# Moving the conditional expert tiles to the middle of the loop, splitting all operands of the dense layer ahead of it, and swapping its two passes

## The chip, the cores and the metric

The kernel runs on one core of a Trainium2 chip. TensorE (PE) multiplies and transposes, VectorE (DVE), ScalarE (ACT) and GpSimd (POOL) work on tiles in SBUF and PSUM, and SyncE (SP) issues nearly all DMA. Each engine works through its own instructions in order; semaphores order the engines among each other. The metric is the time of one execution on the device in microseconds (us). TensorE's clock has two levels here, 1.2 and 2.4 GHz; the profile gives the granted clock as a share of the upper one.

## The reference

1792 tokens (4 sequences of 448) of width 768 pass through three parts in float32:

```
scores = q @ k^T / 8 - log(448);  attn = sigmoid(scores);  x = attn @ v    # 12 heads of 64
e = argmax(x @ w_gate);  g = softmax(x @ w_gate)[e]                        # 8 experts
y = g * (relu(x @ w1[e]) @ w2[e])                                          # 768 -> 1024 -> 768
h = y @ w_in;  out = (h * sigmoid(h)) @ w_out                              # 768 -> 2048 -> 768
```

Which expert a token takes depends on the inputs, so the number of tokens of each expert is known only while the kernel runs. w_in and w_out are float64 (read as pairs of 32-bit words) and are turned into float32 on the chip, called decoding here: a `Square` on ScalarE and four operations on VectorE for each piece of 128 x 768.

## The kernel before, in words

Matrices that want float32 accuracy are split in two parts, high and low (names ending in `h` and `l`), and each product is three matmuls. A split is a cast on ScalarE and a subtraction on VectorE (a few on GpSimd).

**Experts.** Tokens are sorted by expert and padded to tiles of 128. The loop has 21 positions (`TMAX`); 14 are needed whatever the inputs (`TMIN`), the rest stand under a branch. With these inputs 19 tiles are live; tiles 0 to 13 are unconditional, 14 to 18 ran under branches, and the branch of position 19 left the loop. In one position TensorE runs 36 matmuls of the first layer (`l1`) in two halves, transposes, and 48 of the second (`l2`). After the first half and 9 more matmuls of the other one it needs ScalarE's `relu` (`hs`), later `hl` from VectorE. When the next tile has another expert, its weights are split: w1 (`split1`) at the end of the position, w2 (`split2`, five pieces and then three) early in the next, and SP starts the loads of the expert after that into `stage1` (3 MB) and `stage2`. The experts change ahead of tiles 4, 5, 6, 10, 11, 13 and 16. `EARLY` says behind which tiles pieces of w_out are decoded (`early`); results go to `Wo` in HBM through two slabs of `sqp`, in turn. `yout` scales the tile's result (`ys`) and stores it to `Yd`.

**The dense layer.** It runs in two passes over tokens, before 768 tokens in pass 0 (two columns of blocks, 384 each) and 1024 in pass 1 (512 each; a pass of W tokens here means blocks W wide), each of eight blocks j over the inner width of 2048. A block has seven products (`prod`, 9 matmuls each) by a scheme that needs seven block products for a 2 x 2 block matrix, then the output half (`ystep`). The seven operands `x` are sums and differences of token rows, transposed. They are made in chunks of 128 columns by `xprep` (gather the rows from `Yd`, transpose, add, split, `put` to `T0` or `T1` in HBM) and loaded from there. For pass 0 three chunks ran behind tiles 11, 12 and 13, with 9 puts each: two of the seven operands were split there, and the other five put whole and split at the head of the dense layer (`xsplit`, `xa`). `xprep1` made pass 1's chunks during pass 0, and `wdecode` the four pieces of w_out left by `EARLY`. `wiload` and `woload` load a block's weights (`wf`, `wof`), `wisplit` and `wosplit` split them.

All of it is recorded in the order in which the code is written (`manual_schedule`), so each engine's queue is the order of the calls; SP's queue holds loads and stores in the same way, and a store that waits for its data holds up the loads written behind it.

Of the kernel before, what the change touches and what calls it, by code (L numbers as in the profile page):

```python
# [2 lines left out]

# [41 lines left out]
WS = 384, 512  # L45
MB = 0, 6
# [13 lines left out]
def attn_moe_ffn(ctx: ExitStack, tc, qT, kT, v, wg, w1, w2, w_in, w_out, out):  # L60
# [21 lines left out]
    T0 = dp.tile([9, 128, KH, WS[0]], F32, name="T0")  # L82
# [8 lines left out]
    pg_t = cp.tile([128, TMAX], F32, name="pg_t")  # L91
    tbl = cp.tile([128, 3, TMAX], I32, name="tbl")
# [61 lines left out]
    gp = M1.pool("m_g", 2)  # L154
    gs4 = M1.pool("m_s", 4)
# [224 lines left out]
    def choose():  # L380
# [17 lines left out]
        nc.vector.tensor_scalar(out=pg_t[:, 0:1], in0=es, scalar1=float(PG), scalar2=None, op0=ALU.mult)  # L398
# [38 lines left out]
    def tables(pn):  # L437
        t3 = lambda n, w=TMAX: c2.tile([128, w, E], F32, name=n)
        t2 = lambda n, w=TMAX: c2.tile([128, w], F32, name=n)
        b3 = lambda t, w=TMAX: t.unsqueeze(1).to_broadcast([128, w, E])  # L440
        b2 = lambda t, w=TMAX: t.unsqueeze(2).to_broadcast([128, w, E])
# [43 lines left out]
        ge, oh = t3("ge"), t3("oht")  # L485
        vec.tensor_scalar(out=tcap, in0=iota_t, scalar1=tot[:, 0:1], scalar2=None, op0=ALU.min)
# [4 lines left out]
        vec.tensor_tensor(out=oh, in0=b2(tcap), in1=b3(sa), op=ALU.is_ge)  # L491
        yield 1
        vec.tensor_tensor(out=ge, in0=b2(tcap), in1=b3(se[:, 0]), op=ALU.is_ge)
        yield 1
        vec.tensor_sub(out=oh, in0=oh, in1=ge)
        yield 1
        vec.tensor_tensor(out=ge, in0=oh, in1=b3(wv), op=ALU.mult)
        yield 1
        st = t2("stt")
        vec.tensor_reduce(out=st, in_=ge, axis=AX.X, op=ALU.add)  # L500
        yield 1
        vec.tensor_add(out=pg_t, in0=st, in1=tcap)
# [49 lines left out]
    def prep(t, nt=N):  # L552
        tk = keep(gs4, [128, 1], F32, "tk", t % 4)
        jk = keep(gs4, [128, NPG], F32, "jk", t % 4)
        nc.vector.scalar_tensor_tensor(out=jk, in0=iota_pg, scalar=pg_t[:, t:t + 1], in1=tt_all,
# [4 lines left out]
        gx = keep(gp, [128, DM], F32, "gx", t % 2)  # L560
        nc.gpsimd.indirect_dma_start(out=gx, out_offset=None, in_=Xd[0:nt], in_offset=off,
# [45 lines left out]
    def rload(f):  # L607
        rawload(rawm[f % 2], w_out[:, f], nc.sync)
# [37 lines left out]
    for k in range(0, G + LAG, 2):  # L646
# [25 lines left out]
        for j in (k, k + 1):  # L672
# [93 lines left out]
    def yout(t, py, gg, tk):  # L766
# [37 lines left out]
    ne = ne1 = reg(tbl[0:1, 2, 0:1], (SP,), E - 1)  # L804
# [9 lines left out]
    def gather(m, xt):  # L814
        nr = min(m + E, TMAX) * 128
        g = nc.gpsimd.indirect_dma_start(out=xt, out_offset=None, in_=Yd[0:nr],
                                         in_offset=bass.IndirectOffsetOnAxis(ap=cidx[:, m:m + 1], axis=0),
                                         bounds_check=nr - 1, oob_is_err=False)
        for t in range(nr // 128, len(ydma)):
            tc.declare_no_dep(g.ins, ydma[t].ins, reason="the rows gathered here end before tile t's")  # L820

    def xprep(p, c, ra, rb, tmp, slab, px):
# [15 lines left out]
        def split(i, a):  # L838
            h, l = slab(), slab()
# [214 lines left out]
    def xprep1():  # L1054
# [259 lines left out]
```

## Time and profile before

| | us |
|---|---|
| median of 3 runs | 1077.64 (1077.37 to 1083.63) |
| profiled execution | 1074.67, span 1072.7 |
| PE busy | 1003.3 (94%) |
| DVE busy | 711.3 (66%) |
| ACT busy | 504.4 (47%) |
| POOL busy | 105.6 (10%) |

Attention and routing fill the first 214 us, expert tiles 1 to 18 the time to 571.7, the dense layer the rest. A busy share of 94% for PE counts a matmul at the lower clock as busy for its longer time, so the clock rows have to be read beside it. DMA moved 206 GB/s in the mean; in the expert part and at the change of pass it moved up to twice that.

### The profile page before, as it was taken

The numbers are of one execution on the slowest core, as the hardware profiler recorded it, in microseconds if no ns is written. First come the engines' busy times: TensorE is split into PE (matmuls) and PEld (weight loads), VectorE is DVE, ScalarE is ACT, GpSimd is POOL, SyncE is SP. The second block draws the span as 40 slices with busy tenths as digits, with TensorE's granted clock in tenths as the row PEclk, the third lists the DMA queues.
The fourth block names the chain that finished last, engine by engine and source line by source line (L and its number), as shares of the span: only waits on it lengthen the run. The fifth ranks groups of instructions, "written<-read, shape, count | busy, mean of one in ns | idle before, by whom it ended". The sixth has DMA issues, their size and how long they took to land. (4 is left out here: it accounts for less than half of the span.)

```text
span 1072.7 us, 15464 instructions
## 1 busy us (share of the span) xinstructions
PE 1003.3 (94%) x5410; PEld 846.8 (79%) x5410; DVE 711.3 (66%) x1388; ACT 504.4 (47%) x836; POOL 105.6 (10%) x97
## 2 busy tenths in 40 slices
PE   7999999799999999989996799989897999999996
PEld 4555555689888888878885799979895999988996
DVE  5899985945986496441612578878873366766664
ACT  6677666334873285522622554445442533344231
POOL 1000000411222023120201000100010000000002
PEclk9999999999999999989997799999999999999998
DMA  8989998367996579884816355546489221022202
GB/s 287 317 307 296 362 283 252 105 232 269 348 371 249 180 257 348 268 271 145 280 45 231 123 196 196 179 160 204 143 308 403 82 82 45 37 81 81 82 1 118
DMA packets 87673, 220.59 MB, mean 206 GB/s; under 512 B 9952, under 2 KB 51808, under 8 KB 81696
## 3 DMA queue, kind: packets, MB, share of 16 engines
q1 hardware_dynamic: 81200, 200.21, 53.4%
q0 software_dynamic: 4528, 19.29, 5.3%
q8 instruction: 44, 0.72, 0.3%
q14 instruction: 45, 0.37, 0.1%
q10 hardware_dynamic: 1856, 0.01, 0.1%
HBM read 164.60 MB, written 54.87 MB: 205 GB/s over the span
## 5 line engine op out<-in xcount | busy, mean ns | idle before, releaser
L1204 PE MATMUL y<-wo,gh 128*128 128x384 f32 x448 | 153.3, 342 | 3.0 <-ACT wo L1011 2.9
L1206 PE MATMUL y<-wo,gl 128*128 128x384 f32 x448 | 151.2, 338 | 0.0
L1205 PE MATMUL y<-wo,gh 128*128 128x384 f32 x448 | 150.9, 337 | 0.3 <-DVE wo L1012 0.3
L1215 DVE TENSOR_TENSOR acc<-acc,y 128x384 f32<-128x384 f32 x196 | 102.0, 551 | 23.3 <-PE y L1206 21.9
L758 PE MATMUL y<-w2h,hl 128*128 128x384 f32 x304 | 103.9, 342 | 10.9 <-DVE hl L747 8.8
L756 PE MATMUL y<-w2h,hh 128*128 128x384 f32 x304 | 106.1, 349 | 0.7 <-ACT hh L746 0.7
L757 PE MATMUL y<-w2l,hh 128*128 128x384 f32 x304 | 103.1, 339 | 3.7 <-POOL w2l L726 2.1
L236 ACT ACTIVATE a<-s,bias 128x896 f32<-128x896 f32 x96 | 82.8, 913 | 46.3 <-PE s L233 43.7
L731 PE MATMUL h<-w1h,xh 128*128 128x512 f32 x228 | 92.7, 407 | 0.6 <-issue 0.3
L733 PE MATMUL h<-w1h,xl 128*128 128x512 f32 x228 | 90.8, 398 | 0.4 <-DVE xl L714 0.4
L732 PE MATMUL h<-w1l,xh 128*128 128x512 f32 x228 | 90.6, 397 | 0.0
L1204 PEld LDWEIGHTS y<-wo,gh 128*128 128x128 f32 x448 | 84.8, 189 | 6.0 <-ACT wo L1011 3.4
L1004 DVE TENSOR_TENSOR wl<-wf,wh 128x384 fp32r<-128x384 f32 x110 | 60.7, 553 | 37.8 <-ACT wh L1003 37.8
L1206 PEld LDWEIGHTS y<-wo,gl 128*128 128x128 f32 x448 | 84.7, 189 | 1.2 <-DVE gl L1117 1.2
L1205 PEld LDWEIGHTS y<-wo,gh 128*128 128x128 f32 x448 | 84.8, 189 | 1.0 <-DVE wo L1012 0.7
L249 PE MATMUL o<-a,vf 128*64 128x448 f32 x384 | 83.0, 554 | 0.0
L747 DVE TENSOR_TENSOR hl<-x,hh 128x512 fp32r<-128x512 f32 x38 | 26.2, 689 | 84.2 <-ACT hh L746 76.1
L758 PEld LDWEIGHTS y<-w2h,hl 128*128 128x128 f32 x304 | 57.7, 190 | 13.7 <-DVE hl L747 10.9
L757 PEld LDWEIGHTS y<-w2l,hh 128*128 128x128 f32 x304 | 57.8, 190 | 5.3 <-POOL w2l L726 2.7
L1117 DVE TENSOR_TENSOR gl<-sg,gh 128x384 fp32r<-128x384 f32 (+1 forms) x64 | 40.0, 626 | 31.9 <-ACT gh L1115 30.4
L756 PEld LDWEIGHTS y<-w2h,hh 128*128 128x128 f32 x304 | 57.8, 190 | 0.9 <-ACT hh L746 0.9
L1115 ACT CAST gh<-sg 128x384 fp32r<-128x384 f32 (+1 forms) x64 | 36.3, 567 | 45.6 <-DVE sg L1114 45.6
(279 smaller groups left out, 2107.1 us busy)
## 6 DMA issues: line engine op xcount, KB each, us to landing
stage<-w SPq DMA_DIRECT2D x14, 1536.0 KB
wf<-Wi SPq DMA_DIRECT2D x15, 1344.0 KB
stage<-w SPq DMA_DIRECT2D x8, 1920.0 KB
stage<-w_in SPq DMA_DIRECT2D x16, 768.0 KB
wof<-Wo SPq DMA_DIRECT2D x16, 768.0 KB
T<-sl SPq DMA_DIRECT2D x56, 192.0 KB
stage<-w SPq DMA_DIRECT2D x8, 1152.0 KB
xb<-T SPq DMA_DIRECT2D x12, 768.0 KB
```

The lines of the kernel that those rows point to most:

```text
L236: nc.scalar.activation(out=a[:, 0:n], in_=ps[:, 0:n, 0:S], func=AF.Sigmoid, bias=bias, scale=1.0 / math.sqrt(D))
L249: nc.tensor.matmul(out=po[pr][r, 0:S], lhsT=vf[:, g, r], rhs=a[:, i if n == 2 else 0], start=(g == 0), stop=(g == NG - 1))
L731: nc.tensor.matmul(out=ph, lhsT=xh[:, k], rhs=w1h[:, k, cs], start=(k == 0), stop=False)
L732: nc.tensor.matmul(out=ph, lhsT=xh[:, k], rhs=w1l[:, k, cs], start=False, stop=False)
L733: nc.tensor.matmul(out=ph, lhsT=xl[:, k], rhs=w1h[:, k, cs], start=False, stop=(k == KC - 1))
L756: nc.tensor.matmul(out=o, lhsT=hh[:, c], rhs=w2h[:, f, ys], start=(f == 0), stop=False)
L757: nc.tensor.matmul(out=o, lhsT=hh[:, c], rhs=w2l[:, f, ys], start=False, stop=False)
L758: nc.tensor.matmul(out=o, lhsT=hl[:, c], rhs=w2h[:, f, ys], start=False, stop=(f == FC - 1))
L1204: nc.tensor.matmul(out=o, lhsT=gh[:, cs], rhs=w_[:, f, 0, ys], start=st, stop=False)
L1205: nc.tensor.matmul(out=o, lhsT=gh[:, cs], rhs=w_[:, f, 1, ys], start=False, stop=False)
L1206: nc.tensor.matmul(out=o, lhsT=gl[:, cs], rhs=w_[:, f, 0, ys], start=False, stop=sp)
L1215: nc.vector.tensor_add(out=a, in0=a, in1=o)
```

## The change

- The conditional positions move to 7 to 13 (`TF` to `TG`). With these inputs positions 7 to 11 hold tiles 7 to 11, position 12's branch jumps to position 14, and positions 14 to 20 hold tiles 12 to 18. The tables of tiles come in two parts, the second (8 wide) for positions from 13 on; at position 14 the state of the loop is set anew from it.
- `EARLY`: 3, 3 and 2 pieces behind tiles 1, 2 and 3, and 3 behind position 14 (tile 12); 11 in all, before 12. Three buffers for raw pieces instead of two.
- Pass 0 has blocks of 512, pass 1 of 384. Pass 0's operands are made in four chunks behind positions 15 to 18 (tiles 13 to 16), all seven split, with 14 puts each from a ring of eight slabs, of which a chunk takes ten. x0 and x1 are loaded at the end of position 19, `wf` and x2 to x4 inside position 20, where the first block's w_in is split too; x5, `wof` and x6 follow the loop.
- The special first block with `xsplit` goes. Pass 0's background work is one chain, five decodes and then three chunks for pass 1, each chunk with two slabs and one buffer of rows.

```diff
-WS = 384, 512
-MB = 0, 6
+WS = 512, 384
+MB = 0, 8
 NJ = F2C // 2
 NA = F2C
 KH = KC // 2
 HK = KH * 128
-EARLY = {1: 2, 2: 2, 3: 1, 6: 2, 7: 2, 8: 2, 9: 1}
+EARLY = {1: 3, 2: 3, 3: 2, 14: 3}
 NM = sum(EARLY.values())
-XPT = TMIN - 3
+NL = TMAX - TMIN
+TF = TMIN - NL
+TG = TMIN
+TP = TG + 2
+XPT = TG + 1
+NX = WS[0] // 128
...
+        yield from lookup(0, TP)
+        vec.tensor_scalar(out=tbl[0][:, 1], in0=iota_t[:, 0:TP], scalar1=float(NL), scalar2=tot[:, 0:1],
+                          op0=ALU.add, op1=ALU.is_le)
...
+        yield from lookup(1, NL + 1)
...
     def early():
         f = len(done)
         sq = sqp[:, 2 + f % 2]
-        for _ in decode(rawm[f % 2], sq, btm):
+        for _ in decode(rawm[f % 3], sq, btm):
             pass
         done.append(sq)
         nc.sync.dma_start(out=Wo[f], in_=sq)
-        if f + 2 < NM:
-            rload(f + 2)
+        if f + 3 < NM:
+            rload(f + 3)
...
-        def split(i, a):
-            h, l = slab(), slab()
+        def split(i, a, l=None):
+            h = slab()
+            l = slab() if l is None else l
             nc.scalar.copy(out=h.bitcast(F32R), in_=a)
             put(2 * i, h)
             nc.vector.tensor_sub(out=l.bitcast(F32R), in0=a, in1=h)
             put(2 * i + 1, l)
 
-        def whole(i, a):
-            if p:
-                split(i, a)
-            else:
-                put(2 + i, a)
-
-        a21, s1, s2, s3, s4 = tmp
+        a21, s1, s2, s4 = tmp
         for r, t in ((ra, ta), (rb, tb)):
             nc.vector.tensor_copy(out=tokq[:, t:t + 1], in_=r[:, DM:YW])
         q = tr(rb, 0, 0)
         nc.scalar.copy(out=a21, in_=q)
         yield 1
         q = tr(rb, 1, 1)
-        if p:
-            split(5, q)
-            yield 1
-        else:
-            a22 = slab()
-            nc.scalar.copy(out=a22, in_=q)
-            put(7, a22)
+        split(5, q)
+        yield 1
         nc.vector.tensor_add(out=s1, in0=a21, in1=q)
-        yield 2
+        yield 1
         q = tr(ra, 0, 0)
         split(0, q)
         yield 1
         nc.vector.tensor_sub(out=s2, in0=s1, in1=q)
         yield 1
-        nc.vector.tensor_sub(out=s3, in0=q, in1=a21)
+        nc.vector.tensor_sub(out=a21, in0=q, in1=a21)
         yield 1
         q = tr(ra, 1, 1)
+        free()
         split(1, q)
         yield 1
         nc.vector.tensor_sub(out=s4, in0=q, in1=s2)
         yield 1
-        for i, a in ((2, s2), (3, s3), (4, s1), (6, s4)):
-            whole(i, a)
-            yield 1
+        for i, a in ((2, s2), (3, a21), (4, s1), (6, s4)):
+            split(i, a, a)
+            yield 1
...
+    def xload(p, i):
...
+        for h in range(2):
+            nc.sync.dma_start(out=hl[h].bitcast(F32), in_=(T0, T1)[p][2 * i + h].rearrange("p k m -> p (k m)"))
...
-        if t >= TMIN:
-            live = reg(tbl[0:1, 1, t:t + 1], (PE, ACT, DVE, SP, POOL), 1)
+        late = t >= TG
+        if TF <= t < TG:
+            live = reg(tbl[0][0:1, 1, t:t + 1], (PE, ACT, DVE, SP, POOL), 1)
             ifs.enter_context(tc.If(live > 0))
+        if t == TG:
+            ifs.close()
+            cur, nxt = prep(t, late=True, rows=False), prep(t + 1, late=True)
+            fr = reg(tbl[1][0:1, 0, 1:2], (ACT, DVE, SP, POOL), 1)
+            ne = reg(tbl[1][0:1, 2, 1:2], (SP,), E - 1)
...
+            if t == TMAX - 1:
+                M1.close()
+                L0.close()
+                F1 = Group("left")
+                wp, xpa = F1.pool("f_w", 1), F1.pool("f_xa", 1)
+                wiload(0)
+                for i in (2, 3, 4):
+                    xps[i] = xpa
+                    xo[0][i] = xload(0, i)
+                wops = [*wisplit()]
...
-        if XPT <= t < TMIN:
+        if XPT <= t < XPT + NX:
             for _ in xg:
                 pass
-        if t == XPT - 2:
-            nc.sync.dma_start(out=sqp[:, 0], in_=Wi[0, :, 0:DM])
-        if t == XPT - 1:
-            wi0 = xr_p[1].tile([128, 2, DM], F32R, tag="xr", name="wi0")
-            nc.scalar.copy(out=wi0[:, 0], in_=sqp[:, 0])
-            nc.vector.tensor_sub(out=wi0[:, 1], in0=sqp[:, 0], in1=wi0[:, 0])
-        if XPT - 1 <= t < TMIN - 1:
+        if XPT - 1 <= t < XPT + NX - 1:
             c = t + 1 - XPT
             rows = ot_p[1].tile([128, 2, YW], F32, tag="ot", name=f"rows{c}")
             gather(c, rows[:, 0])
-            gather(KH + c, rows[:, 1])
-            sl8 = sqp.rearrange("p n (a c) -> p (n a) c", a=2)
-            slabs = iter([sl8[:, i] for i in (5, 6, 7, 0, 5)])
-            xg = xprep(0, c, rows[:, 0], rows[:, 1], [sl8[:, i] for i in range(5)],
+            gather(NX + c, rows[:, 1])
+            if c == 0:
+                sl8 = sqp.rearrange("p n (a c) -> p (n a) c", a=2)
+                sl4 = xr_p[1].tile([128, 4, HK], F32, tag="xr", name="sl4")
+                ring = [sl8[:, i] for i in range(4, 8)] + [sl4[:, i] for i in range(4)]
+                slabs = cycle(ring)
+            xg = xprep(0, c, rows[:, 0], rows[:, 1], [sl8[:, i] for i in range(4)],
                        lambda: next(slabs), lambda i: keep(ps_t, [128, 384], F32, f"t{i}", 0))
...
+        if t == XPT + NX:
             for i in range(2):
...
+                xo[0][i] = xload(0, i)
...
+    for i in (5, 6):
+        xps[i] = xpb
+        xo[0][i] = xload(0, i)
+        if i == 5:
+            woload(0)
...
-    wiload(0, True, 2, 3)
-    xland(0)
-    wiload(0, False, 3, 5)
-    xland(1)
-    xland(2)
-    wiload(0, False, 5, 7)
-    xland(3)
-    xland(4)
-    woload(0)
...
-    def xsplit(i):
-        t = xp0.tile([128, 2, KH, W], F32R, tag=f"x{i}", name=f"xa{i}")
-        src = land[i].rearrange("p (k m) -> p k m", k=KH)
-        for k in range(KH):
-            nc.scalar.copy(out=t[:, 0, k], in_=src[:, k])
-            nc.vector.tensor_sub(out=t[:, 1, k], in0=src[:, k], in1=t[:, 0, k])
-        xo0.append([[t[:, h, k] for k in range(KH)] for h in range(2)])
...
+    bgs = chain(wdecode(), xprep1())
...
-            first = p == 0 and j == 0
             nx = not (p == 1 and last)
-            if nx and not first:
+            if nx:
                 wiload((j + 1) % NJ)
                 woload((j + 1) % NJ)
             g = {}
             wo = wosplit()
-            ex = wisplit(2) if first else None
-
-            def start(i):
-                if first:
-                    wops.append(next(ex))
-                    xsplit(i - 2)
             prod(0, x, True)
             c1 = tmp("c1")
             nc.scalar.copy(out=c1, in_=x)
-            if first:
-                start(2)
-            else:
-                next(wo)
+            next(wo)
             prod(1, y, True)
             nc.vector.tensor_add(out=c1, in0=c1, in1=y)
             g11 = gate(0, c1)
             next(g11)
             next(g11)
-            if first:
-                start(3)
             prod(2, x, False)
             c2_ = tmp("c2")
             nc.scalar.copy(out=c2_, in_=x)
-            if first:
-                start(4)
-            else:
-                w_ = next(wo)
+            w_ = next(wo)
+            bg(p)
             prod(3, z, True)
             z7 = tmp("z7")
             nc.scalar.copy(out=z7, in_=z)
-            if first:
-                start(5)
-            else:
-                bg(p, j)
-                if p == 0:
-                    next(wd, 0)
+            bg(p)
             prod(4, x, False)
             nc.vector.tensor_add(out=z7, in0=z7, in1=x)
             g22 = gate(3, z7)
             next(g22)
-            if first:
-                start(6)
             prod(5, z, False)
...
-                for _ in xg:
+                for _ in bgs:
                     pass
-                Q0.close()
-                xp1 = Q1.pool("f_x1", 1)
-                for i in (2, 0, 1, 3, 4, 5, 6):
-                    xo1[i] = xload1(xp1, i)
+                for i in range(7):
+                    xo[1][i] = xload(1, i)
             ws = wisplit() if nx else iter(())
```

ScalarE's queue from the weight split behind tile 12 on (`w1h` casts; `L855` to `L840` are a chunk of `xprep`), to the `relu` (`hs`) of tile 13, before:

```order
L719 CAST w1h<-stage_86 128x1024 x6
L919 UNCONDITIONAL_BRANCH x2
L769 ACTIVATE ys_2500<-y_2385,gg_2059 128x768
L855 COPY w_96<-t_0_2190 128x384
L863 COPY w_96<-t_0_2191 128x384
L840 CAST w_96<-t_0_2190 128x384
L840 CAST w_96<-t_0_2191 128x384
L896 COMPARE_AND_BRANCH
L724 CAST w2h<-stage_100 128x768 x5
L896 UNCONDITIONAL_BRANCH x2
L737 ACTIVATE hs_2253<-h_2229 128x512
```

The same place, behind tile 12, in the change (position 14):

```order
L741 CAST w1h<-stage_88 128x1024 x6
L981 UNCONDITIONAL_BRANCH x2
L112 ACTIVATE w_98<-rawm_2387 128x768
L112 ACTIVATE w_98<-rawm_2386 128x768
L112 ACTIVATE w_98<-w_98 128x768
L791 ACTIVATE ys_2529<-y_2392,gg_2717 128x768
L947 COMPARE_AND_BRANCH
L746 CAST w2h<-stage_102 128x768 x5
L947 UNCONDITIONAL_BRANCH x2
L759 ACTIVATE hs_2255<-h_2231 128x512
```

Three `Square` of decodes (into slabs of `w_98`, which is `sqp`) stand where four steps of a chunk stood.

ScalarE's queue behind position 17 (tile 15), up to the splits of w2 for tile 16, in the change; before, `ys` stood next to the casts of `w2h` here:

```order
L741 CAST w1h<-stage_88 128x1024 x6
L981 UNCONDITIONAL_BRANCH x2
L791 ACTIVATE ys_2529<-y_2392,gg_2533 128x768
L873 COPY w_98<-t_0_2192 128x384
L864 CAST sl_5215<-t_0_2193 128x384
L864 CAST sl_5215<-t_0_2192 128x384
L864 CAST w_98<-t_0_2193 128x384
L864 CAST w_98<-w_98 128x384 x2
L864 CAST sl_5215<-w_98 128x384 x2
L947 COMPARE_AND_BRANCH
L746 CAST w2h<-stage_102 128x768 x5
L947 UNCONDITIONAL_BRANCH x2
```

A chunk of eight ScalarE steps (`L873` and seven casts of `L864`) now stands between the two weight splits of the change to tile 16.

SP's queue from the last live position on, before (`acc` is where five whole operands land):

```order
L770 DMA Yd<-ys_2500 128x769
L962 UNCONDITIONAL_BRANCH x8
L991 DMA wf_6338<-Wi 128x384
L1023 DMA acc<-T_65 128x1152
L991 DMA wf_6338<-Wi 128x768
L1023 DMA acc<-T_65 128x1152 x2
L991 DMA wf_6338<-Wi 128x768
L1023 DMA acc<-T_65 128x1152 x2
L995 DMA wof_0_6347<-Wo 128x2x768
L991 DMA wf_6512<-Wi 128x2688
L995 DMA wof_1_6514<-Wo 128x2x768
```

And in the change, from position 20's loads on:

```order
L914 DMA wf_6401<-Wi 128x2688
L909 DMA x_2_6403<-T_65 128x1536 x2
L909 DMA x_3_6406<-T_65 128x1536 x2
L909 DMA x_4_6409<-T_65 128x1536 x2
L792 DMA Yd<-ys_2529 128x769
L909 DMA x_5_6526<-T_65 128x1536 x2
L1036 DMA wof_0_6529<-Wo 128x2x768
L909 DMA x_6_6531<-T_65 128x1536 x2
L914 DMA wf_6537<-Wi 128x2688
```

The load of `wf` and three operands moved ahead of the last tile's store to `Yd`; that of `wof_0` stands behind all of them and behind x5.

## Rows read from the trace of the kernel before

**Rows 1.** The page, busy time by engine: us, share, instructions.

```profile
PE 1003.3 (94%) x5410; PEld 846.8 (79%) x5410; DVE 711.3 (66%) x1388; ACT 504.4 (47%) x836; POOL 105.6 (10%) x97
```

**Rows 2.** Stretches: length; busy PE, PEld, DVE, ACT, POOL; PEclk, DMA share, GB/s.

```profile
214.50:571.70 357.20, 342.06 (x1800) 304.15 (x1800) 205.57 (x321) 168.80 (x251) 66.27 (x49) 0.99 0.69 246
329.48:347.78 18.30, 18.30 (x99) 16.54 (x99) 10.39 (x18) 5.74 (x9) 2.00 (x2) 1.00 0.58 200
426.87:448.72 21.85, 20.04 (x114) 17.81 (x112) 13.15 (x23) 11.42 (x17) 4.00 (x4) 1.00 0.78 237
515.24:534.89 19.65, 18.57 (x99) 16.50 (x99) 13.14 (x19) 9.90 (x16) 4.04 (x3) 1.00 0.98 348
269.85:290.16 20.31, 18.81 (x99) 16.42 (x99) 20.10 (x26) 16.54 (x23) 5.89 (x3) 1.00 0.99 368
571.70:620.70 49.00, 33.37 (x145) 29.71 (x146) 21.67 (x43) 24.32 (x53) 4.01 (x4) 0.76 0.51 190
620.70:804.40 183.70, 174.35 (x985) 167.21 (x985) 148.54 (x286) 85.48 (x177) 10.12 (x9) 1.00 0.59 201
804.40:845.90 41.50, 34.24 (x162) 29.36 (x161) 15.05 (x24) 17.87 (x35) 1.07 (x2) 0.96 0.64 263
845.86:877.04 31.18, 31.18 (x161) 28.46 (x161) 19.90 (x35) 11.48 (x22) 0.00 (x0) 1.00 0.19 71
860.26:877.04 16.78, 16.78 (x98) 16.62 (x97) 12.98 (x26) 4.64 (x10) 0.00 (x0) 1.00 0.01 1
...
448.72:478.59 29.87, 24.61 (x114) 21.15 (x112) 12.47 (x25) 11.60 (x19) 7.40 (x6) 0.83 0.86 301
```

**Rows 3.** Timeline, change of expert in tile 4: start, us, engine, line, operation [idle before].

```profile
270.02 0.90 ACT L106 ACTIVATE w<-rawm 128x768 f32<-128x768 f32 x1
...
271.61 3.77 ACT L724 CAST w2h<-stage 128x768 fp32r<-128x768 f32 x5
...
272.27 0.55 DVE L107 TENSOR_SCALAR btm<-rawm 128x768 int32<-128x768 int32 x1
...
275.85 4.42 DVE L726 TENSOR_TENSOR w2l<-stage,w2h 128x768 fp32r<-128x768 f32 x5
...
280.93 0.44 PE L758 MATMUL y<-w2h,hl 128*128 128x384 f32 x1 [1.09 <-DVE hl L747]
```

**Rows 4.** Stretch behind tile 13's gap, columns as in rows 2.

```profile
460.80:469.40 8.60, 5.00 (x17) 4.91 (x18) 6.71 (x12) 2.71 (x4) 3.51 (x3) 0.60 0.99 336
```

**Rows 5.** Timeline, ahead of and in tile 13 (SPq is SP's issuing).

```profile
444.33 3.74 SPq L923 DMA_DIRECT2D stage<-w  x2
...
448.81 13.60 SPq L829 DMA_DIRECT2D T<-w  x9
...
458.36 0.56 DVE L842 TENSOR_TENSOR w<-t,w 128x384 fp32r<-128x384 f32 x1 [8.61 <-DMA T<-w]
...
464.40 0.69 PE L758 MATMUL y<-w2h,hl 128*128 128x384 f32 x1 [3.63 <-DVE hl L747]
```

**Rows 6.** Groups of ScalarE in a free 512 block: busy us, mean ns | idle before.

```profile
L1115 ACT CAST gh<-sg 128x512 fp32r<-128x512 f32 x4 | 2.5, 621 | 3.1 <-DVE sg L1114 3.1
L1011 ACT CAST wo<-wof 128x768 fp32r<-128x768 f32 x2 | 1.7, 837 | 0.0
```

**Rows 7.** Timeline of TensorE, the gaps from the last tile through the first dense block.

```profile
573.22 0.42 PE L1103 MATMUL X<-f,wi 128*128 128x384 f32 x1 [1.56 <-ACTq L962]
...
583.87 0.69 PE L1103 MATMUL X<-xa,wh 128*128 128x384 f32 x1 [7.27 <-ACT xa L1050]
...
604.14 0.69 PE L1204 MATMUL y<-wo,gh 128*128 128x384 f32 x1 [2.90 <-ACT wo L1011]
```

**Rows 8.** Stretch at the change of pass, columns as in rows 2.

```profile
801.00:826.00 25.00, 19.01 (x76) 14.45 (x74) 9.81 (x17) 5.63 (x9) 3.16 (x3) 0.93 1.02 423
```

**Rows 9.** Waits in the block around the change of pass: total us, times, longest.

```profile
PE Y L1104 <- DMA xb1l<-T: 2.9, 1, 2.9
```

**Rows 10.** Timeline of VectorE, one step of the tables of tiles.

```profile
198.80 0.33 DVE L493 TENSOR_TENSOR ge<-tcap,se 128x168 f32<-128x168 f32 x1
```

More of the change, by code (lines that the diff above doesn't have):

```diff
@@ L2 @@
 from contextlib import ExitStack
+from itertools import chain, cycle
 import concourse.bacc as _bacc
@@ new lines, in lookup @@
+        def lookup(i, w):
+            yield from member(oh, tcap, w)
+            yield from total(st, oh, wv, w)
+            vec.tensor_add(out=pg_t[i], in0=st[:, 0:w], in1=tcap[:, 0:w])
+            yield "pg"
+            yield from total(et, oh, iota_e, w)
+            yield from total(sx, oh, se[:, 0], w)
+            vec.memset(tbl[i][:, 0, 0:1], 0.0)
+            yield 1
+            vec.tensor_tensor(out=tbl[i][:, 0, 1:], in0=et[:, 1:w], in1=et[:, :w - 1], op=ALU.not_equal)
+            yield 1
+            yield from member(ge, sx, w)
+            yield from total(et, ge, iota_e, w)
+            vec.tensor_copy(out=tbl[i][:, 2], in_=et[:, 0:w])
+            yield 1
@@ L560, in prep @@
         gx = keep(gp, [128, DM], F32, "gx", t % 2)
+        if not rows:
+            return gx, gi, tk
         nc.gpsimd.indirect_dma_start(out=gx, out_offset=None, in_=Xd[0:nt], in_offset=off,
@@ L607, in rload @@
     def rload(f):
-        rawload(rawm[f % 2], w_out[:, f], nc.sync)
+        rawload(rawm[f % 3], w_out[:, f], nc.sync)
     def early():
@@ L794, in attn_moe_ffn @@
     rawm = [ot_p[1].tile([128, DM, 2], I32, tag="ot", name="rawm0"),
-            sqp[:, 0:2].rearrange("p n d -> p (n d)").bitcast(I32).rearrange("p (n w) -> p n w", w=2)]
+            sqp[:, 0:2].rearrange("p n d -> p (n d)").bitcast(I32).rearrange("p (n w) -> p n w", w=2),
+            xr_p[1].tile([128, DM, 2], I32, tag="xr", name="rawm2")]
     btm = c2.tile([128, DM], I32, tag="xf", name="btm")
-    rload(0)
-    rload(1)
+    for f in range(3):
+        rload(f)
     py = psy(0)
@@ L978, in attn_moe_ffn @@
     sgp = F.pool("f_s", 2)
-    Q0, Q1 = Group("left"), Group("left")
-    xs = Q0.pool("f_xs", 1)
-    xl_ = Q0.pool("f_sl", 4)
-    xp0 = Q0.pool("f_x0", 1)
+    xs_t = F.pool("f_xs", 1).tile([128, 2 * YW + 4 * HK], F32, name="xs_t")
+    xsl = F.pool("f_sl", 2)
     PF = ExitStack()
@@ L996, in woload @@
         wos.append(t)
[L998 to L1005 removed]
     def wosplit():
         t = wos.pop(0)
[L1009 removed]
+        w = wp1.tile([128, 2, 2, DM], F32R, tag="wo", name=f"wo{len(wfs)}")
         for f in (1, 0):
@@ L1056, in xprep1, with fetch @@
         n = WS[1] // 128
-        tmp = [xs_t[:, 4 * YW + i * HK:4 * YW + (i + 1) * HK] for i in range(5)]
-        def rows(c):
-            for i in range(2):
-                gather(MB[1] + n * i + c, base[:, 2 * (c % 2) + i])
-        rows(0)
+        rows = [xs_t[:, i * YW:(i + 1) * YW] for i in range(2)]
+        tmp = [xs_t[:, 2 * YW + i * HK:2 * YW + (i + 1) * HK] for i in range(4)]
+        def fetch(c):
+            if c < n:
+                for i in range(2):
+                    gather(MB[1] + n * i + c, rows[i])
@@ L1085, in attn_moe_ffn @@
-    wops = [[wi0[:, h, i * HK:(i + 1) * HK] for h in range(2)] for i in range(2)]
+            yield from xprep(1, c, *rows, tmp, lambda: xsl.tile([128, HK], F32, tag="sl", name="sl"),
+                             lambda i: ps_t.tile([128, HK], F32, tag="t", name="ft"), lambda: fetch(c + 1))
     bank = [ps_h.tile([128, 512], F32, tag=t, name=t) for t in "XYZ"]
     X, Y, Z = (t for t in bank)
-    xg, wd = xprep1(), wdecode()
-    xo1 = {}
+    bgs = chain(wdecode(), xprep1())
     def ffn2(p):
@@ L1181, in ffn2 @@
             next(g12)
-            if first:
-                next(wo)
-                w_ = next(wo)
-                wiload(1)
-                woload(1)
             if p == 0 and last:
-                for _ in xg:
+                for _ in bgs:
                     pass
-                Q0.close()
-                xp1 = Q1.pool("f_x1", 1)
-                for i in (2, 0, 1, 3, 4, 5, 6):
-                    xo1[i] = xload1(xp1, i)
+                for i in range(7):
+                    xo[1][i] = xload(1, i)
             ws = wisplit() if nx else iter(())
@@ L1222, in yend @@
                     tc.add_to_no_dep_group("out", sc.ins)
-                if p == 0 and j > 0 and t % nt:
-                    next(wd, 0)
                 nw.extend(x_ for x_ in [next(ws, None)] if x_)
-                bg(p, j)
+                bg(p)
             def ytile(t, s):
@@ L1249, in ffn2, with bg @@
             wops = nw
-    def bg(p, j):
+    def bg(p):
         if p == 0:
-            next(xg, 0)
+            next(bgs, 0)
     ffn2(0)
```

223 lines of the change are left out of this document (94 added, 129 removed).

## Prediction

> **What bounds the kernel now.** The top rows first: TensorE is busy 94% of the span and VectorE 66% [rows 1], so a change can save only where TensorE waits or runs at its lower clock. A table by stretches [rows 2] shows where. An expert tile with nothing beside it takes 18.30 us, all of it matmuls; tiles 1 to 18 took 357.2 us, 27.8 more than 18 such tiles. A free dense block of 512 tokens takes 31.18 us (14.4 for the seven products, 16.78 for the output half), so by columns a free one of 384 takes about 23.4. The stretch from the last expert tile through the first dense block took 49.0 us, 25.6 too many; the next seven blocks 183.7 us, 19.9 too many, with VectorE busy 148.5 us of them, 21.2 us a block; the block around the change of pass 41.5 us, 10.3 too many. These four excesses are what the change can touch. I then read what TensorE waited for in them.
>
> The long gaps come with a second price. In those 49.0 us the granted clock was 0.76 of the 2.4 GHz level, which is 11.8 us lost to stretches at 1.2 GHz behind the gaps there [rows 2, 7]; from tile 13's gap of 3.63 us on, a stretch of 8.6 us ran at 0.60 and lost 3.4 us [rows 4, 5]. I price a long gap at its length plus 3 us.
>
> **The change, part by part.** I sum against the profiled execution, 1074.67 us (its span is 1072.7), 3.0 below the median of the runs, 1077.64, and put the result on that median.
>
> *Expert tiles, more decodes.* The `EARLY` table puts two decodes instead of one behind tile 3, ahead of the change of expert in tile 4. VectorE's queue there is last weight splits, decode (272.27 to 275.85, 3.6 us), five splits of w2 (4.42), `hl`; TensorE starts on that `hl` at 280.93 after waiting 1.09 us [rows 3], so it wanted it 10.0 us into the tile, which began at 269.85 [rows 2]. No cover is left, so the second decode costs 3.6 us, and a gap of 4.7 us brings most of a clock loss, 2.4. Tile 4 goes from 2.0 over to 8.0. Tiles 5, 6, 10 and 11 change expert with no decode; such a change is 19.65 us, 1.35 over [rows 2], together 5.4.
>
> *Tile 13, the three decodes at position 14.* VectorE: 3 x 3.6 = 10.8 us between the two weight splits, from about 1 us before the tile begins, then 4.4 of w2 and `hl` at about 15; TensorE wants `hl` at 10. ScalarE is worse. Its third `Square` writes the slab from which the first decode's result is being stored to HBM, and that store stands on the queues behind the 3 MB of `stage1`. Behind the Square on ScalarE (0.90 us) are the `ys` product, five casts (3.77 [rows 3]) and the `relu`, for which TensorE waits after 27 of the 36 first-layer matmuls, by columns 6.5 us into the tile. Behind such a load (two issues from 444.33) a small store issued from 448.81 on was waited for until 458.36, for 8.61 us [rows 5]. A store done 5 us into the tile would mean a stall of about 6, one done at 10 us a stall of about 10; I take 9, nearer the row, plus 3 of clock: 12, between 8 and 14.
>
> *Four chunks of operand preparation.* Before, three chunks; the one with no collision made tile 12 21.85 us, 3.55 over [rows 2]. After, four, each with 14 puts for 9. More copies on ScalarE and VectorE, but the transposes that TensorE waits for are spaced by the same few copies, so 3.55 each: 14.2 (between 10 and 20). Tile 13's old collision (29.87 us, 11.6 over [rows 2], `hl` late behind a put) disappears, but the same thing is built again: chunk 2 now ends position 17, ahead of the change into tile 16, with `stage1`'s load in front of its puts. Its last two copies on ScalarE reuse the slabs of its first two puts, so ScalarE waits for those to land, about 9.5 us after issue by the old case. Issued 3 us into the tile they would hold the five casts until 12.5 and the `relu` until 18, a stall of 11.5; VectorE's wait before ended in one of 3.63 [rows 5]. Nearer the upper end, because the blocked engine now feeds the `relu`: 9, plus 3 of clock, plus 1.35 of the change: 13.4 (between 5 and 16).
>
> *The jump.* The branch over unused positions moves from the end into the loop. Its gap was 1.56 us [rows 7]; I leave it at 1.6. The Trainium skill (Runtime: NRT & Kernel Launch, section on instruction fetch mechanics) says that a taken branch to a target outside the loaded window stalls for a fetch, which speaks against a jump at a place where five engines follow each other. The trace's one such jump shows the 1.56.
>
> Expert part after: 8.0 + 5.4 + 12 + 13.4 + 14.2 + 1.6 = 54.6 over, against 27.8: **+26.8 us**. The longer table work before tile 1 (some 25 VectorE operations like one of 0.33 us [rows 10]) lies beside tile 1's first matmuls; without that cover it would cost 8.
>
> *Transition.* Removed: waits for `xa` (the longest 7.27 us) and for `wo` (2.90) [rows 7], as operands come split and early. Late next is the load of w_out's rows, `wof`: on the queue behind x0 and x1 (3.15 MB), `wf` (1.38), x2 to x4 (4.72), a tile's rows (0.39) and x5 (1.57), with its own 0.79 12.0 MB. At the 423 GB/s that a saturated stretch moved [rows 8] this is 28.4 us, from some 3 us after position 19 ends; position 20 covers 18.3, so it lands 13.4 us into the dense block. ScalarE meets the cast of `wo` second: c1 copy, `wo` cast (0.84), sigmoid, `gh` (0.62), c2 copy [rows 6], with VectorE's product between: five steps, some 3.9 us with their hand-overs. TensorE's fifth product overwrites what the c2 copy reads, so it starts at about 17.3 instead of 4 x 2.06 = 8.2: 9.1 idle, 3 of clock, 0.6 of small waits, 12.7 instead of 25.6: **-13**. If `wof` were first on that queue this would be -23; at the worst, with `wf` late too, 0. The Trainium skill (SBUF — State Buffer, section Summary: rules for kernel authors) would have HBM transfers estimated at 358 GB/s; the rows show 423, and the measurement decides. By the rule `wof` would land 5 us later and this term be -8.
>
> *Pass 0.* VectorE had 21.2 us of work in blocks of 23.4. With 512 tokens a block has 19.9 of its own [rows 2] and about 4 of background (one decode more, one chunk fewer, eight blocks to spread over), 24 of 31.2. Slack grows from 2 to 7 us a block; I let the loss fall from 2.8 to 1.1 us a block: 8 x 1.1 = 9 against 19.9, **-11** (between 0 and -18).
>
> *Change of pass.* TensorE waited 2.9 us for an operand load [rows 9] and lost more around it. The loads shrink to 14 x 0.59 = 8.3 MB, 19.5 us at 423 GB/s, beside 16.78 us of output half, and the products that use them one after another are spaced 14.4 x 0.75 / 7 = 1.54 us. The last lands at about 22, wanted at 26. **-9** (between 0 and -10). Pass 1 with 384 tokens has nothing in the background: 0.
>
> Sum: 26.8 - 13 - 11 - 9 = -6.2, so 1071.4 us.
>
> **Rivals.** *Slower, 0.21:* ScalarE's waits on its own stores are the rule, not the exception. Position 14 then costs 14 and chunk 2 15, and chunk 0 too, which runs while the loads of the change in tile 13 still move, costs 9 more; chunks 1 and 3 are 5 each. Expert part: 8.0 + 5.4 + 14 + 1.35 + 15 + 4 x 3.55 + 9 + 3 + 1.6 = 71.6, so +43.8 - 33 = +10.8, at 1088.5, and 1094 with a clock loss of its own at chunk 0. It decides if a put of 192 KB lands over 8 us after issue in position 15 as well. For it speaks the row of 8.61 us; against it that a slab comes round only after seven other copies. *Faster, 0.29:* stores land between loads within some 3 us. Then tile 13 is 8 over, tile 16 5, chunks 2.5 each (10), expert part 38, +10: -23, at 1055. For it: the DMA engines were busy only 0.69 of the expert part [rows 2]. *The loads do not hide, 0.13:* the transition stays at 25 since x2 to x4 wait for weights' space; -6 + 13 = +7, 1084. *Position 14's jump refetches on all engines, 0.04:* the wait of TensorE at it becomes some 7 us, as the longest gap of this kind of hand-over in the transition, 7.27; 1077.
>
> **Numbers.** My forecast, 0.33, is 1071.5, itself between 1062 and 1081. The range goes from 1050 (faster case with pass 0 fully freed) to 1094. About 1%, 10.8 us, is what a measurement of this kernel can tell from no change. Faster by more than that (below 1067): 0.29 x 0.9 + 0.33 x 0.25 = 0.34. Slower (above 1088): 0.21 x 0.65 + 0.13 x 0.3 + 0.33 x 0.05 = 0.19. Same: 0.47.
>
> **What would show it.** Tile 4 at 26 us with a gap of 4 to 5 for `hl`; the tile after position 14 at about 30 with ScalarE waiting for a store of `Wo`; tile 16 at about 32 with ScalarE waiting for a put; the first dense block at about 44 with one gap before the fifth product, behind the cast of `wo`; pass 0's later blocks near 32.3; no gap over 1 us at the change of pass. I would be wrong if ScalarE's waits on stores are short (faster) or if pass 0's blocks stay 2 us over (slower).

## The result, and the profile after

The change made the kernel slower: 1092.95 us median (1092.01 to 1093.93, 4 runs), ratio 1.0128 to the kernel before, 95% interval [1.0092, 1.0164]. I had forecast 1071.5 and a small gain. The spans of the two profiled executions are 1072.7 and 1091.6 us; the 18.9 us between them are what the rows below share out. Between the medians lie 15.3 us, mostly because the profiled execution before was 3.0 below its median. Each row is one execution: in the other kernels below that leave these tiles alone, tile 3 took 20.6 to 23.4 us, tile 13 34.3 to 35.4 and tile 16 33.5 to 33.9, so a difference of 1 us, in tile 3 of 2 or 3, says little.

The stretches of the kernel after that answer to [rows 2]: tiles 1 to 18; tile 3, tile 4, tile 13, tile 15, tile 16; the first dense block; the seven after it; the block around the change of pass (the first of pass 1); a free block of 384. Columns as there.

```profile
215.19:602.43 387.24, 347.34 (x1807) 307.95 (x1807) 219.12 (x365) 175.32 (x268) 65.74 (x50) 0.96 0.70 245
252.69:275.17 22.48, 19.88 (x100) 17.59 (x99) 13.48 (x19) 10.28 (x14) 3.04 (x2) 0.92 0.69 251
275.17:300.91 25.74, 21.59 (x99) 18.95 (x99) 23.14 (x31) 17.19 (x24) 4.38 (x3) 0.87 0.99 370
...
453.96:489.62 35.66, 23.13 (x111) 19.73 (x111) 25.12 (x36) 14.87 (x23) 7.26 (x5) 0.81 0.73 266
511.24:533.50 22.26, 20.04 (x113) 17.77 (x112) 15.20 (x28) 13.16 (x21) 4.30 (x4) 1.00 0.78 233
533.50:566.45 32.95, 21.99 (x113) 18.83 (x112) 16.33 (x29) 13.23 (x23) 8.01 (x7) 0.90 0.86 298
602.43:651.35 48.92, 33.18 (x160) 29.30 (x160) 19.62 (x32) 21.42 (x43) 0.00 (x0) 0.86 0.62 244
651.35:881.16 229.81, 224.60 (x1150) 202.45 (x1150) 171.17 (x306) 90.99 (x170) 14.03 (x13) 1.00 0.44 147
881.16:915.69 34.53, 27.70 (x137) 25.11 (x136) 11.50 (x20) 14.00 (x29) 0.98 (x1) 0.90 0.70 287
915.69:939.62 23.93, 23.77 (x136) 23.45 (x136) 16.38 (x31) 11.09 (x24) 0.00 (x0) 1.00 0.24 91
```

The last row is the free block of 384 tokens that the kernel before did not show: 23.93 us, not the 23.4 that I had scaled from columns. With it, the time over free tiles and blocks (a free tile 18.30, a free 512 block 31.18) reads:

| stretch | before | forecast after | after |
|---|---|---|---|
| tiles 1 to 18 | 27.8 | 54.6 | 57.8 |
| first dense block | 25.1 | 12.7 | 17.7 |
| next seven blocks | 16.2 | 9 | 11.6 |
| change of pass | 10.3 | 1 | 10.6 |

The expert part lost 30.0 us, the other three gave 11.7 back where I had counted on 33. The remaining 0.6 lies ahead of tile 1.

What TensorE, ScalarE and SP did at the four places, from timelines of the kernel after (start, us, engine, line, operation [idle before <- what ended it]). Tile 13, behind position 14's decodes:

```profile
464.64 0.91 ACT L112 ACTIVATE w<-w 128x768 f32<-128x768 f32 x1 [8.58 <-DMA Wo<-w]
...
466.23 3.75 ACT L746 CAST w2h<-stage 128x768 fp32r<-128x768 f32 x5
469.89 0.59 ACT L759 ACTIVATE hs<-h 128x512 f32<-128x512 f32 x1
```

```profile
460.19 7.61 SPq L638 DMA_DIRECT2D Wo<-w  x3
```

```profile
470.53 0.69 PE L765 MATMUL x<-ident,hs 128*128 128x128 f32 x2 [10.12 <-ACT hs L759]
```

The third `Square` waits 8.58 us for the store out of the slab that it writes; casts and `relu` queue behind it, and TensorE stands for 10.12 us. The store itself took less than that: SP issued it at 460.19, when VectorE's first decode was done, and the `Square` could start at 464.64, 4.4 us later. Ahead of tile 16 the same pattern appears with a chunk's puts:

```profile
543.08 1.06 ACT L864 CAST sl<-w 128x384 fp32r<-128x384 f32 x2 [7.99 <-DMA T<-sl]
```

```profile
532.06 0.34 SPq L985 DMA_DIRECT2D stage<-w  x1
...
533.49 6.23 SPq L852 DMA_DIRECT2D T<-sl  x4
```

The chunk's first put was issued at 533.49 and the copy that reuses its slab could start at 543.08, 9.6 us later; TensorE waited 8.31. The first dense block:

```profile
622.04 0.83 ACT L1043 CAST wo<-wof 128x768 fp32r<-128x768 f32 x1 [15.53 <-DMA wof<-Wo]
```

```profile
605.88 0.32 SPq L792 DMA_DIRECT2D Yd<-ys  x1
613.98 0.80 SPq L909 DMA_DIRECT2D x<-T  x2
614.87 0.38 SPq L1036 DMA_DIRECT2D wof<-Wo  x1
```

```profile
627.10 0.79 PE L1098 MATMUL X<-x,wh 128*128 128x512 f32 x1 [15.74 <-ACT c L1135]
```

The one gap is where I put it, before the fifth product and behind the cast of `wo`, but 15.74 us long instead of 9.1. SP stands still from 605.9 to 613.98, and its waits say for what:

```profile
SPq L909 <- DMA Yd<-ys: 7.7, 1, 7.7
```

x5 is loaded into space that the last tile's result leaves, so its load waits until that result is stored; the store stands behind x2 to x4 on the queues, and `wof` behind x5 on SP. At the change of pass:

```profile
869.05 0.60 SPq L852 DMA_DIRECT2D T<-xs_t  x1
869.74 1.08 SPq L909 DMA_DIRECT2D x<-T  x2
```

```profile
PE X L1099 <- DMA x<-T: 3.2, 2, 2.3
```

```profile
898.87 0.45 PE L1099 MATMUL Z<-x,wh 128*128 128x384 f32 x1 [0.92 <-DMA x<-T]
```

```profile
q0 software_dynamic: 640, 3.15, 26.0%
```

Pass 1's loads start at 869.74, right behind the last chunk's last put, although the last product that reads the old operands ended at 863.5. They also took long: at 898.87, 29.1 us after their first issue, TensorE still waited for the twelfth of the 14 loads (the second half of x5). The last row is of the DMA between these two times (packets, MB, share of the engines): beside the loads GpSimd's queue moved 3.15 MB, pass 0's own output rows (`out`, 1024 tokens of 3 KB).

### The profile page after: what moved, and what is told of

Same layout as the page of the kernel before. It is cut to its first block, busy times and chain, and to the rows that moved or that the text cites. A ratio compares the mean times of both kernels' runs of the same rounds, so it can differ in the third digit from the quotient of the medians.

```text
span 1091.6 us, 15509 instructions
## 1 busy us (share of the span) xinstructions
PE 1000.3 (92%) x5404; PEld 846.0 (77%) x5404; DVE 717.1 (66%) x1410; ACT 501.8 (46%) x832; POOL 103.3 (9%) x96
## 5 line engine op out<-in xcount | busy, mean ns | idle before, releaser
L1098 PE MATMUL X<-x,wh 128*128 128x512 f32 (+1 forms) x192 | 72.2, 376 | 17.5 <-ACT c L1135 16.9
L1099 PE MATMUL X<-x,wh 128*128 128x512 f32 (+1 forms) x192 | 70.7, 368 | 3.2 <-DMA x<-T 3.2
L1100 PE MATMUL X<-x,wl 128*128 128x512 f32 (+1 forms) x192 | 70.9, 369 | 0.0
L1044 DVE TENSOR_TENSOR wo<-wof,wo 128x768 fp32r<-128x768 f32 x32 | 30.7, 958 | 58.2 <-ACT wo L1043 58.2
L780 PEld LDWEIGHTS y<-w2h,hl 128*128 128x128 f32 x304 | 57.8, 190 | 13.2 <-DVE hl L769 7.9
```

Source lines behind the costliest of these rows:

```text
L780: nc.tensor.matmul(out=o, lhsT=hl[:, c], rhs=w2h[:, f, ys], start=False, stop=(f == FC - 1))
L1098: nc.tensor.matmul(out=ps, lhsT=h[:, ks], rhs=xh, start=start and k == 0, stop=False, skip_group_check=skip)
L1100: nc.tensor.matmul(out=ps, lhsT=l[:, ks], rhs=xh, start=False, stop=k == KH - 1, skip_group_check=skip)
```

## The experiments

Each of the first four kernels takes one of these waits away, by another place, another buffer or another order. The theory (A) is that these are four separate waits of an engine or queue for a transfer that stands behind others; the rival (B) that they cover for one another, so that taking one away only shows the next. (Together they cost more than the 18.9 us, because the change had won time beside them.)

**Three decodes behind position 6.**

```diff
-EARLY = {1: 3, 2: 3, 3: 2, 14: 3}
+EARLY = {1: 3, 2: 3, 3: 2, 6: 3}
```

> The three decodes of position 14 are moved behind position 6, where no change of expert follows. Theory A (the wait belongs to the place: three decodes and a store behind the load of stage1, between the two weight splits of tile 13): tile 13 falls from 35.7 us to about 23 (change 1.35, chunk 3.3 over 18.3); tile 7 pays 0 to 4 us as tile 3 does for its three decodes (22.5 us there). Sum -8 to -12.5, so 1080.5 to 1085 against 1092.95. Theory B (waits only move: chunk 0 and the loads of the change hold tile 13 anyway): tile 13 stays over 30 us, at most -4.

1080.87 us, ratio 1.0031 [1.0007, 1.0055], against 1.0128. Tile 13 and tile 7 of this kernel:

```profile
451.19:474.08 22.89, 20.22 (x111) 17.63 (x111) 14.86 (x24) 12.18 (x20) 5.14 (x4) 1.00 0.92 346
337.19:355.74 18.55, 18.49 (x100) 16.44 (x100) 9.85 (x17) 4.83 (x8) 1.99 (x2) 1.00 0.34 127
```

Tile 13 gains 12.8 us and the clock does not fall; tile 7 pays 0.25 here, and 0.8 to 2.6 in the three later kernels with these decodes. A holds. Three decodes cost little there, where no weights are split and no big load stands on the queues.

**Ring of ten slabs.**

```diff
+                ring += [btm[:, i * HK:(i + 1) * HK].bitcast(F32) for i in range(2)]
                 slabs = cycle(ring)
```

> Two more slabs for the chunks (from the decoding buffer, which is free by then), so that no copy of a chunk waits for a put of the same chunk. Theory A: ScalarE's 8.0 us wait ahead of tile 16 goes, its relu comes about 8 us earlier, tile 16 falls from 32.95 us to 24 or 25: -8, so 1085. Theory B (the puts and stage2's load stand in the same order behind stage1's load, and the next wait in line, for w2 or a slab of the chunk after, takes over): at most -3.

1084.22 us, ratio 1.0056 [1.0031, 1.0081]. Tile 16:

```profile
530.22:553.63 23.41, 20.55 (x113) 17.66 (x112) 15.97 (x29) 13.15 (x23) 8.34 (x7) 1.00 1.05 361
```

9.5 us less, at full clock, with the same puts and loads on the queues. The wait for the slab was the cost.

**Rows of w_out first.**

```diff
+    woload(0)
     for i in (5, 6):
         xps[i] = xpb
         xo[0][i] = xload(0, i)
-        if i == 5:
-            woload(0)
```

> The load of the first block's rows of w_out is issued right behind the loop, ahead of x5, whose load waits for the last tile's store. Theory A (the cast of wo is late because its load stands in SP's queue behind that wait): the load lands at about 616 instead of 622, the gap before the fifth product falls from 15.7 us to 9 or 10, the first dense block from 48.9 to 42 or 43: -6, so 1087. Theory B (the 12 MB on the queues set the time whatever the order): at most -2, or x5 becomes the late one and nothing is won.

1086.02 us, ratio 1.0072 [1.0049, 1.0095]. The first dense block and SP's issues:

```profile
598.70:641.22 42.52, 33.14 (x161) 29.77 (x161) 18.86 (x31) 20.71 (x42) 0.00 (x0) 0.88 0.71 278
```

```profile
582.72 0.82 SPq L909 DMA_DIRECT2D x<-T  x2
...
601.41 0.32 SPq L792 DMA_DIRECT2D Yd<-ys  x1
601.84 0.38 SPq L1036 DMA_DIRECT2D wof<-Wo  x1
609.54 1.97 SPq L909 DMA_DIRECT2D x<-T  x4
```

```profile
611.46 0.83 ACT L1043 CAST wo<-wof 128x768 fp32r<-128x768 f32 x1 [9.41 <-DMA wof<-Wo]
```

```profile
616.51 0.79 PE L1097 MATMUL X<-x,wh 128*128 128x512 f32 x1 [9.38 <-ACT c L1134]
```

`wof` is now issued 0.4 us after the store, 7.7 us ahead of x5; the gap is 9.38 us and the block 42.5, as A had it. That is near what my prediction gave (9.1, 43.9), but not its case: there x5 stood in front of `wof`, here it stands behind. The edit takes away x5's wait and x5's 1.57 MB at once, and does not separate the two.

**One more background step a block.**

```diff
             nc.vector.tensor_add(out=c1, in0=c1, in1=y)
+            bg(p)
             g11 = gate(0, c1)
```

> One more step of pass 0's background chain in each block, so that the last chunk's puts are over before the last block's products end. Theory A (pass 1's loads start 6.2 us late because SP's queue holds the last puts in front of them): loads start at about 863.5 instead of 869.7, the first block of pass 1 falls from 34.5 us to 25 to 27: -7 to -9; pass 0's blocks pay up to 1 us more. So 1085. Theory B (the loads take longer than the output half that covers them, 8.26 MB at some 360 GB/s in 23 us against 17.7): at most -3.

1078.05 us, ratio 1.0007 [0.9983, 1.0031]. The block around the change of pass and the seven blocks ahead of it:

```profile
876.32:900.26 23.94, 23.77 (x136) 23.45 (x136) 11.30 (x20) 13.72 (x29) 0.98 (x1) 1.00 0.37 135
650.59:876.32 225.73, 223.76 (x1150) 202.83 (x1150) 169.75 (x306) 91.24 (x170) 13.60 (x13) 1.00 0.50 178
```

The change of pass costs nothing any more: 10.6 us gained, more than forecast, and 4.1 in pass 0, where I had expected to pay. With all puts over before the last block, the loads start at 847.43, each as soon as its operand's last reader is done:

```profile
841.39 0.51 SPq L852 DMA_DIRECT2D T<-xs_t  x1
...
847.43 0.81 SPq L909 DMA_DIRECT2D x<-T  x2
```

Theory A had them start when the last product ends; they started 12.1 us before that (it ended at 859.5). So the run shows that the loss goes with an earlier start, and leaves B's point open: with a start at the end of the products the loads might still have been too long for the output half.

In pass 0 the chunks' transposes on TensorE show most of the 4.1 us. The rows are of the seven blocks in the kernel before, the kernel after and this one (busy us, mean ns | idle before):

```profile
L834 PE MATMUL ft<-ident,xs_t 128*128 128x128 f32 x39 | 6.5, 276 | 5.9 <-DVE xs_t L872 3.5 <-issue 1.8 <-PE y L1206 0.5
L857 PE MATMUL ft<-ident,xs_t 128*128 128x128 f32 x36 | 6.1, 278 | 4.3 <-issue 2.9 <-DVE xs_t L885 1.0 <-DMA xs_t<-Yd,cidx 0.3
L857 PE MATMUL ft<-ident,xs_t 128*128 128x128 f32 x36 | 5.9, 273 | 1.6 <-DVE xs_t L885 1.6
```

The idle time in front of them falls from 4.3 to 1.6 us; the steps fall at other points of a block. What made the rest was not separated.

**A third slab for the third decode**, to test whether ScalarE or VectorE held tile 13:

```diff
         sq = sqp[:, 2 + f % 2]
+        if f == 10:
+            sq = rawm[2].rearrange("p n w -> p (n w)")[:, 0:DM].bitcast(F32)
```

> Of position 14's three decodes only the third changes: it is written into a third slab (the raw buffer that the first decode has emptied), so its Square need not wait for the first decode's store. Theory A (my prediction's step: ScalarE's wait for that store, 8.6 us, is what holds the relu and so tile 13): the relu comes 8 us earlier and tile 13 falls from 35.7 us to 27 or 28. Rival (VectorE's three decodes, 10.9 us, and the splits of w2 behind them end at 472 either way, so hl is late on its own account): TensorE's 10.1 us wait for the relu only turns into one of about 8 us for hl, and tile 13 stays between 32 and 34.5 us.

1087.93 us in its only execution. Tile 13 took 31.04 us, between the two; TensorE's two waits there, and the third `Square`:

```profile
462.86 1.11 PE L767 MATMUL x<-ident,hs 128*128 128x128 f32 x4 [4.65 <-ACT hs L761]
470.29 0.44 PE L782 MATMUL y<-w2h,hl 128*128 128x384 f32 x1 [1.65 <-DVE hl L771]
```

```profile
456.96 0.91 ACT L112 ACTIVATE rawm<-w 128x768 f32<-128x768 f32 x1 [3.12 <-issue]
```

10.12 us become 4.65 and 1.65. ScalarE's wait for the store held the tile, as predicted, but only for 4.6 us of the tile's 12.8 that went when the decodes moved; below it lie two more limits, VectorE's own `hl` and a wait of 3.12 us that the `Square` still has. The profile names no releaser for that one; the `Square` starts when VectorE's last read of the raw buffer that it writes ends (at 456.88). So the remedy is to move the decodes, not to add a slab.

**All four together, and two further steps.**

> The edits of the four kernels before together: three decodes behind position 6, ring of ten slabs, load of wo's rows ahead of x5, one more background step. If the four waits are independent (theory A), the gains in their own places add: 12.8 in tile 13, 9.5 in tile 16, 6.4 in the first dense block, 10.6 at the change of pass, less 1: -38 against 1092.95, so 1055. If one takes over from another (theory B), two thirds of it at most: 1067 or more.

1050.54 us, ratio 0.9771 [0.9734, 0.9808]. The four single gains, as differences of ratio from 1.0128, are 0.0097, 0.0072, 0.0056 and 0.0121, together 0.0346; all four gave 0.0357. As each difference carries the uncertainty of 1.0128 (0.0036 either way), the sum alone would not exclude B's two thirds. The places do; tiles 13 and 16, the first dense block and the change of pass in this kernel:

```profile
454.51:477.42 22.91, 20.23 (x111) 17.64 (x111) 14.86 (x24) 12.19 (x20) 5.12 (x4) 1.00 0.92 345
521.25:544.65 23.40, 20.53 (x114) 17.65 (x112) 15.98 (x29) 13.15 (x23) 8.33 (x7) 1.00 1.05 362
580.62:622.88 42.26, 33.16 (x160) 29.76 (x160) 18.88 (x31) 20.42 (x41) 0.00 (x0) 0.88 0.72 286
848.63:872.58 23.95, 23.78 (x137) 23.46 (x137) 11.30 (x20) 13.73 (x29) 0.99 (x2) 1.00 0.38 133
```

They are 12.8, 9.6, 6.7 and 10.6 us shorter than in the kernel after, against 12.8, 9.5, 6.4 and 10.6 singly. The waits are independent, and B falls.

```diff
-EARLY = {1: 3, 2: 3, 3: 2, 6: 3}
+EARLY = {1: 2, 2: 2, 3: 1, 4: 1, 5: 1, 6: 3, 14: 1}
```

> As the kernel with all four, and the eleven decodes spread: 2, 2, 1, 1, 1, 3 behind tiles 1 to 6 and 1 behind position 14, so that no change of expert has more than one decode ahead of it. Theory A (a decode ahead of a change costs its 3.6 us of VectorE beyond the slack, one decode 0.65 us as in tile 4 before: 20.31 against 19.65): tiles 3 and 4 fall from 22.5 and 25.75 us to 18.3 and 20.3, tiles 5, 6 and 13 pay 0.65 each: -7.5, so about 1047. Rival (these tiles wait for loads of raw pieces or weights rather than VectorE): at most -3.

1043.84 us, ratio 0.9693 [0.9664, 0.9723]. Tiles 3, 4 and 13:

```profile
252.12:270.40 18.28, 18.28 (x100) 16.53 (x100) 9.95 (x15) 9.51 (x13) 1.99 (x2) 1.00 0.52 176
270.40:290.74 20.34, 18.83 (x100) 16.44 (x100) 20.13 (x26) 16.95 (x24) 6.23 (x3) 1.00 1.00 372
446.56:470.34 23.78, 20.55 (x111) 17.52 (x111) 17.96 (x28) 13.06 (x21) 5.15 (x3) 1.00 0.92 345
```

Tile 3 is free and tile 4 as before the change; tiles 5, 6 and 13 pay 0.9 to 1.0 each, a little more than the 0.65 expected. The median fell by 6.7 us of the 7.5 expected, so the rival (at most 3) falls.

```diff
-                for i in (2, 3, 4):
+                for i in (2, 3):
...
-    for i in (5, 6):
-        xps[i] = xpb
+    for i in (4, 5, 6):
+        xps[i] = xpa if i == 4 else xpb
```

> As the kernel before it, and x4's load moves behind the first load of wo's rows, so that these stand in front of 3.15 MB more. Theory A (order on SP's queue decides): those rows land about 4 us earlier, the gap before the fifth product falls from 9.4 us to 4 to 6, with the clock -4 to -6, so 1042. Rival (the queue's total holds: x5 or x6 becomes the late one): the gap moves to a later product, at most -2.

1041.81 us, ratio 0.9678 [0.9649, 0.9706]; the interval overlaps that of the kernel before it, so of the two the runs do not say which is faster, and the 4 to 6 us expected are not shown: the medians differ by 2.0. The first dense block went from 43.6 to 39.85 us and the gap from 9.61 to 5.88, still before the fifth product:

```profile
576.91:616.76 39.85, 33.91 (x160) 29.51 (x160) 19.27 (x32) 20.95 (x42) 0.00 (x0) 0.91 0.76 304
```

The last two kernels both beat the kernel before the change by 3%.

## Why the prediction was wrong

The forecast was -6.2 us and the traces show +18.9 (the medians +15.3). By its own terms:

- **Expert part, +26.8; measured +30.0.** Right in mechanism and nearly in size. Tile 4: 8.0 over forecast, 7.4 measured. Tile 13: a stall of 9 forecast, 10.12 measured. Chunk 2: a put landing 9.5 us after issue, 9.6 measured; a stall of 9, 8.31 measured. A chunk 3.55, measured 3.3 to 4.0 (tiles 14 and 15). (The sum leaves out the 1.35 us of tile 13's change of expert, and the signs, 30 and 32 us for tiles 13 and 16, leave out the chunk that the sum has there; by the sum they are 33.9 and 35.3, measured 35.66 and 32.95.) The jump: 1.6, measured 1.04. The Trainium skill's rule on taken branches (Runtime: NRT & Kernel Launch, section on instruction fetch mechanics) would have it stall if its target lies outside the loaded window; the trace shows no more than that 1.04 us. Missed: tile 3, 4.2 over. I had costed the third decode behind tiles 1 and 2 at nothing, without naming its cover; its Square waited 10.11 us for the store of its own slab, the wait that I had seen at position 14 and not here:

```profile
259.25 0.89 ACT L112 ACTIVATE w<-rawm 128x768 f32<-128x768 f32 x1 [10.11 <-DMA Wo<-w]
```

- **Change of pass, -9; measured +0.3.** The largest failure. I set 19.5 us of loads against 16.78 us of cover as if the loads began with the output half and had the DMA engines to themselves. On SP's queue the last chunk's puts stand in front of them, and these wait for the background chain, which the last block only then flushes: the loads began 6.2 us after even the last product. By my own sum that alone would make the last load some 2 us late (22 + 6.2 against 26). But the loads took 29.1 us up to the twelfth of 14, while pass 0's output rows, 3.15 MB that the sum left out, moved beside them. In the fourth experiment the loads began 12.1 us ahead of the last product's end and the loss was gone; how much of it a start at that end would have left, no run shows.
- **Transition, -13; measured -7.4.** The right load and the right product, mis-sized. From x0's issue to the cast of `wo` the kernel after took 35.6 us (586.45 to 622.04), against 28.4 in the sum. I left out that x5, in front of `wof`, waits for the last tile's store to free its space. And the rate was too high: in the third experiment, where that wait and x5 are out of the way, 10.4 MB up to `wof` would be 24.7 us at 423 GB/s, and the trace has 28.7 (582.72 to 611.46). So 4.0 of the 7.2 us are the rate, and the slower one that I set aside would have come nearer. That experiment's gap, 9.38 us against the 9.1 worked out, agrees by luck: with x5 behind `wof` the sum would have given about 5.4. (A slip in the sum: 28.4 + 3 - 18.3 is 13.1, not 13.4.)
- **Pass 0, -11; measured -4.6.** Of the 6.4 missing, 3.7 are no loss at all but my free 384 block, too short by 0.53 us in each of seven; the rest is 11.6 us left in place of 9 (which I summed over eight blocks, where the stretch has seven). I had priced the whole loss as VectorE's lack of slack. Of the 11.6 us, 6.1 are TensorE's own transposes for the chunks and 4.3 its waits in front of them, against 6.5 and 5.9 before; no slack of VectorE takes the transposes away. The waits fell to 1.6 with one more step a block, which does not change VectorE's work.

Three gains were sized too large, each from a view that showed the removed wait and not all that took its place. The slower rival named a wait of the same kind, ScalarE's waits on its own stores, and at 1088.5 came out near the measured time, but by luck: it kept the three gains, and its extra loss in chunk 0 did not happen (tile 14 was 3.3 over).

## What to carry to other kernels

A slab that is written again ties its engine to the landing of a store, and with a weight load on the queues the engine stood for 8 to 10 us here: give a burst as many slabs as it writes, or move it to where no load runs. Before a load is called hidden, read its queue from the instruction in front of it backwards: what that one waits for (space, a store, another engine's step) sets the start, and only then do bytes and rates count, with those of every other transfer that runs beside it. Measure the free unit of each size in the trace before calling the rest a loss.

## What the runs showed of the hardware that was not expected

A put of 192 KB issued at 533.49 landed by 543.08, although the load just ahead of it, 1.57 MB issued at 532.06, would be 3.7 us at 423 GB/s. The queues held more than that: the other half of those weights had been issued at 528.65, and a tile's rows and GpSimd's gathers were under way too. Between the put's issue and its landing the DMA engines had no pause and moved 3.5 MB:

```profile
533.49:543.08 9.59, 6.56 (x30) 4.97 (x28) 3.01 (x7) 1.31 (x3) 2.98 (x3) 1.00 1.01 370
```

And the granted clock came back when the waits went: the mean over tiles 1 to 18 was 0.96 in the kernel after and 1.00 in the last one, whose same stretch took 362.43 us:

```profile
214.48:576.91 362.43, 341.47 (x1807) 302.13 (x1808) 219.63 (x366) 176.04 (x269) 69.26 (x50) 1.00 0.74 262
```
